# Three-bank score tiles and values in four column groups, in a two-layer transformer on one Trainium2 core

## The chip, the cores and the metric

The kernel runs on one core of a Trainium2 chip. Its engines work from queues of their own: TensorE (PE) multiplies matrices into PSUM, ScalarE (ACT) computes activations, VectorE (DVE) does elementwise work, GpSimd (POOL) copies and clears, SyncE (SP) starts DMAs. The metric is the device time of one execution in microseconds, lower is better. "Start to start" below is the distance of two neighbouring instructions of one engine.

## The reference

All inputs are bfloat16. `x` is 2048 x 512; attention has 32 heads of 16; the feed-forward width is 1792. The same weights are used in both layers.

```python
def A(x, wqkv, wo):                 # B=1, S=2048, D=512, H=32, Dh=16
    q, k, v = split(x @ wqkv)       # (H, S, Dh) each
    p = softmax(q @ k.T * Dh ** -0.5)
    return concat_heads(p @ v) @ wo

def B(x, w1, w2):
    return silu(x @ w1) @ w2

for layer in range(2):
    x = x + A(layernorm(x), wqkv, wo)
    x = x + B(layernorm(x), w1, w2)
return x
```

## The kernel before

Everything lies in SBUF. The 2048 queries are worked in four chunks of 512 (`c`), heads in eight blocks of four (`hb`), keys in 16 tiles of 128 (`kt`). A unit is one `(c, hb, kt)`: 512 in a layer.

For a unit, `emit_s` issues four score matmuls (L520). The four heads of a block lie at partitions 32j to 32j+16 of `KT` and `QT`, 17 rows each, the 17th holding a bound that keeps the exponent small; so the four use four row groups of the array. They write two PSUM tiles of two banks (`wide`, three such tiles in turn). ACT takes each tile with one exponential of 128 x 1024 into `p_sb` (L585). `emit_pv` then issues four value matmuls (L532), one for each head, all adding into one bank `o_ps`: the stationary operand is 128 columns wide and zero but for the head's 17 (16 of V and a column of ones that sums the exponentials). These padded operands, `vd`, are filled by POOL copies (L141), four for every four key tiles. After 16 key tiles DVE copies `o_ps` to `oT` (L573), and a step transposes it back and divides by the sums (`heads_piece`, L336 to L343).

All else in attention is a side step: K and Q of the next head block (`k_piece` L225, `q_piece` L298 to L327), the output projection of the last chunk (`epilogue_pieces` L362, L371), its feed-forward (`ffn_pieces`: L392, tanh L429, gate L430, L399) and the next layer's normalising and V (`next_pieces`, L269). A step has at most two matmuls of 512 columns or four transposes; they share one PSUM bank (`narrow`). A list `Pump` holds the steps, and after each unit some are issued, as many as it takes to be done by the end of the chunk. PE, ACT and DVE run in the order in which the program is written (`manual_schedule`).

The order in a unit is: exponentials of this unit, scores of the next, values of the last half and this first half, side steps. ACT and PE wait for each other through the score tiles.

Ahead of layer 0 stand the normalising, K of block 0, its maximum and Q, and all of V, one after another. Behind each layer's attention the last chunk's projection and feed-forward (`ffn_last`) run by themselves, and behind layer 0 the last chunk's normalising and V, and K of block 0 for all of layer 1.

Of the kernel before, what the change touches and what calls it, by code (L numbers as in the profile page):

```python
# [18 lines left out]
def kernel(  # L19
# [10 lines left out]
    nc = tc.nc  # L30
# [11 lines left out]
    NQC = S // 512  # L42
# [5 lines left out]
    NG = 4  # L48
    NR = 2
# [4 lines left out]
    xnpool = ctx.enter_context(tc.tile_pool(name="xnpool", bufs=2))  # L54
    xtpool = ctx.enter_context(tc.tile_pool(name="xtpool", bufs=4))
    vpool = ctx.enter_context(tc.tile_pool(name="vpool", bufs=2))
    qpool = ctx.enter_context(tc.tile_pool(name="qpool", bufs=3))
    qwork = ctx.enter_context(tc.tile_pool(name="qwork", bufs=1))
    ppool = ctx.enter_context(tc.tile_pool(name="ppool", bufs=5))
# [5 lines left out]
    spool = ctx.enter_context(tc.tile_pool(name="spool", bufs=3, space=bass.MemoryType.PSUM))  # L65
# [3 lines left out]
    def wide(name):  # L69
        return spool.tile([P, 2, 512], FP32, name=name, tag="s")  # L70
# [27 lines left out]

    x_sb = xpool.tile([P, TT, D], BF16, name="x_sb")
    for c in range(NQC):  # L100
        nc.sync.dma_start(
            x_sb[:, 4 * c : 4 * c + 4, :],
            xf[512 * c : 512 * (c + 1), :].rearrange("(tt p) d -> p tt d", p=P),
        )
# [22 lines left out]
    amax = xpool.tile([P, HB], FP32, name="amax")  # L127
    vs = [vpool.tile([P, TT, D], BF16, name=f"v{i}", tag="v") for i in range(2)]
    vdq = []
    for i in range(NR):  # L130
        vd = xpool.tile([P, NG, 4, P], BF16, name=f"vd{i}")
        nc.gpsimd.memset(vd[:], 0.0)
        for j in range(4):
            nc.gpsimd.memset(vd[:, :, j, 32 * j + DH : 32 * j + DH + 1], 1.0)
        vdq.append(vd)


    def vd_fill(va, hb, g, slot):
        for j in range(4):
            h = 4 * hb + j  # L140
            nc.gpsimd.tensor_copy(  # L141
                out=vdq[slot][:, :, j, 32 * j : 32 * j + DH],
                in_=va[:, NG * g : NG * (g + 1), DH * h : DH * (h + 1)],
            )
# [7 lines left out]
    def ln_rstd_act(mvb, rstd, n):  # L152
        std = small.tile([P, n, 1], FP32, name="std", tag="std")
        nc.scalar.activation(std[:], mvb[:, :, 1:2], ACT.Sqrt, bias=eps_t[:], scale=1.0)
        nc.vector.reciprocal(rstd[:], std[:])

    def ln_rstd(mvb, rstd, n):
        va = small.tile([P, n, 1], FP32, name="va", tag="va")
        nc.vector.tensor_scalar_add(out=va[:], in0=mvb[:, :, 1:2], scalar1=float(EPS))
# [6 lines left out]
            out=rstd[:].bitcast(I32), in0=sh[:], scalar1=-1.0, scalar2=float(0x5F3759DF),  # L166
# [4 lines left out]
        for _ in range(3):  # L171
            nc.vector.scalar_tensor_tensor(
                out=t1[:], in0=rstd[:], scalar=-0.5, in1=rstd[:], op0=ALU.mult, op1=ALU.mult
            )
            nc.vector.tensor_tensor(out=t2[:], in0=t1[:], in1=va[:], op=ALU.mult)
            nc.vector.scalar_tensor_tensor(
                out=rstd[:], in0=t2[:], scalar=1.5, in1=rstd[:], op0=ALU.add, op1=ALU.mult
            )
# [9 lines left out]
    def transpose_tile(xn, xnT, tq, wide_ps=False):  # L188
        if wide_ps:
            t_ps = spool.tile([P, CT, P], BF16, name="t4_ps", tag="s")  # L190
        else:
            t_ps = gpool.tile([P, CT, P], BF16, name="t_ps", tag="g")
        for ct in range(CT):
            nc.tensor.transpose(t_ps[:, ct, :], xn[:, ct * P : (ct + 1) * P], ident[:, :])  # L194
        nc.vector.tensor_copy(out=xnT[:, :, tq * P : (tq + 1) * P], in_=t_ps[:, :, :])


    def ln_steps(c, cell, act_sqrt=False, wide_ps=False):
        def stats(pair):
            if pair == 0:  # L200
                cell["mvb"] = small.tile([P, 4, 2], FP32, name="mvb", tag="mvb")
                cell["rstd"] = small.tile([P, 4, 1], FP32, name="rstd", tag="rstd")
            for i in (2 * pair, 2 * pair + 1):
                ln_stats(cell["mvb"], i, 4 * c + i)

        def rs():
            if act_sqrt:
                ln_rstd_act(cell["mvb"], cell["rstd"], 4)
            else:
                ln_rstd(cell["mvb"], cell["rstd"], 4)  # L210
            cell["xn0"] = ln_apply(cell["mvb"], cell["rstd"], 0, 4 * c)

        def tr(tq):
            if tq == 0:
                cell["xnT"] = xtpool.tile([P, CT, 512], BF16, name="xnT", tag="xt")
            if tq < 3:
                cell[f"xn{tq + 1}"] = ln_apply(cell["mvb"], cell["rstd"], tq + 1, 4 * c + tq + 1)
            transpose_tile(cell[f"xn{tq}"], cell["xnT"], tq, wide_ps)

        return [[lambda: stats(0), lambda: stats(1), rs]] + [[lambda tq=tq: tr(tq)] for tq in range(4)]  # L220


    def k_mm(xnT, hb, ps, cts):
        for ct in cts:
# [3 lines left out]
                rhs=xnT[:, ct, :],  # L228
# [4 lines left out]
    def k_piece(xnTs, c, hb):  # L233
        cell = {}

        def a():
            cell["ps"] = narrow("k_ps")
            k_mm(xnTs[c], hb, cell["ps"][:, :], (0, 1))

        def b():  # L240
            k_mm(xnTs[c], hb, cell["ps"][:, :], (2, 3))
            nc.vector.tensor_scalar(  # L242
                out=KT[:, hb, c * 512 : (c + 1) * 512], in0=cell["ps"][:, :],
                scalar1=onescol[:, 0:1], scalar2=None, op0=ALU.add,
            )
# [3 lines left out]
    def k_two(xnTs, c, hb):  # L249
        k_ps = wide("k2_ps")  # L250
        for i in range(2):
            k_mm(xnTs[c + i], hb, k_ps[:, i, :], range(CT))
        nc.vector.tensor_scalar(
            out=KT[:, hb, c * 512 : (c + 2) * 512],
            in0=k_ps[:].rearrange("p a b -> p (a b)"),
            scalar1=onescol[:, 0:1], scalar2=None, op0=ALU.add,
        )

    def amax_bm(hb):
        nc.vector.tensor_reduce(  # L260
            out=amax[:, hb : hb + 1], in_=KT[:, hb, :], axis=AX.X, op=ALU.max,
            apply_absolute_value=True,
        )
        nc.vector.tensor_scalar_mul(out=Bm[:, hb, :], in0=E[:, :], scalar1=amax[:, hb : hb + 1])

    def v_mm(xnT, tt, ps, cts):
        tq = tt % 4
        for ct in cts:
            nc.tensor.matmul(  # L269
                ps, lhsT=xnT[:, ct, tq * P : (tq + 1) * P], rhs=wv_sb[:, ct, :],  # L270
                start=(ct == 0), stop=(ct == CT - 1),
            )

    def v_piece(cellx, tt, va):
        cell = {}

        def a():
            cell["ps"] = narrow("v_ps")
            v_mm(cellx["xnT"], tt, cell["ps"][:, :], (0, 1))

        def b():
            v_mm(cellx["xnT"], tt, cell["ps"][:, :], (2, 3))
            nc.vector.tensor_copy(out=va[:, tt, :], in_=cell["ps"][:, :])

        return [a, b]

    def v_two(xnT, tt, va):
        ps = wide("v2_ps")
        for i in range(2):
            v_mm(xnT, tt + i, ps[:, i, :], range(CT))  # L290
        nc.vector.tensor_copy(out=va[:, tt : tt + 2, :], in_=ps[:, :, :])

    def q_piece(xnTs, c, hb, QTs):
        cell = {}

        def mm(cts):
            for ct in cts:
                nc.tensor.matmul(  # L298
                    cell["ps"][:, :],
                    lhsT=wq_pad[:, ct, 4 * hb : 4 * hb + 4, :].rearrange("p h s -> p (h s)"),  # L300
                    rhs=xnTs[c][:, ct, :],
# [8 lines left out]
        def b():  # L310
            mm((2, 3))
            qc = qwork.tile([P, 512], BF16, name="qc", tag="qc")
            nc.vector.tensor_copy(out=qc[:], in_=cell["ps"][:, :])  # L313
            qu = qwork.tile([P, 512], BF16, name="qu", tag="qu")
            nc.vector.tensor_scalar(
                out=qu[:].bitcast(I16), in0=qc[:].bitcast(I16), scalar1=0x7FFF, scalar2=None,
                op0=ALU.bitwise_and,
            )
            cell["qu"] = qu

        def d():
            nc.tensor.matmul(  # L322
                cell["ps"][:, :], lhsT=Bm[:, hb, :], rhs=cell["qu"][:], start=False, stop=True,
                skip_group_check=True,
            )
            QTs[c][hb] = qpool.tile([P, 512], BF16, name="QT", tag="qt")
            nc.vector.tensor_copy(out=QTs[c][hb][:], in_=cell["ps"][:, :])  # L327

        return [a, b, d]


    def heads_piece(oT, hb, attn):
        def a():
            at_ps = gpool.tile([P, 4, 4, 32], BF16, name="at_ps", tag="g")
            for tq in range(4):
# [6 lines left out]
            nc.vector.reciprocal(rec[:], at_ps[:, :, :, DH : DH + 1])  # L342
            nc.vector.tensor_tensor(  # L343
                out=attn[:, :, 64 * hb : 64 * hb + 64].rearrange("p t (j d) -> p t j d", j=4),
                in0=at_ps[:, :, :, 0:DH],
                in1=rec[:].to_broadcast([P, 4, 4, DH]),
# [5 lines left out]


    def epilogue_pieces(c, attn):
        pieces = []
        for tq in range(4):
# [23 lines left out]
            def pc(tq=tq, cell=cell, mm=mm):  # L380
                mm((2, 3))
                tt = 4 * c + tq
# [7 lines left out]
    def h_mm(xfT, ft, ps, cts):  # L390
        for ct in cts:
            nc.tensor.matmul(  # L392
                ps, lhsT=w1_sb[:, ct, ft * P : (ft + 1) * P], rhs=xfT[:, ct, :],
# [290 lines left out]
```

## Time and profile before

| | us |
|---|---|
| timed runs | 2185.21, 2188.16 (median), 2188.69 |
| span of the profiled execution | 2190.4 |
| to the first exponential | 65.2 |
| attention of layer 0 | 1006.1 |
| last exponential of layer 0 to first of layer 1 | 89.9 |
| attention of layer 1 | 968.3 |
| last exponential to the end | 60.8 |

The profiled execution is listed by its span, from its first instruction to its last; no other time of it is given. It lies 2.2 us above the median of the timed runs. In the page a line of a group gives the engine, the operation, the tiles, shapes and count, then the busy time, the mean duration of one in ns, and the engine's idle time ahead of it with what ended it. A duration counts from issue, so neighbouring ACT or PE instructions overlap in it: 2048 exponentials of 1237 ns are 1920 us busy. `PEclk` is the clock that TensorE was granted, in tenths of full speed for 40 slices of the span. A timeline line has the start, the time to the last end, engine, line and operation, and a count where several were merged. A stretch line has its two ends, its length, the time PE was busy with the count of matmuls, the granted clock, and the DMA share and rate.

### The profile page before, as it was taken

The numbers are of one execution on the slowest core, as the hardware profiler recorded it, in microseconds if no ns is written. First come the engines' busy times: TensorE is split into PE (matmuls) and PEld (weight loads), VectorE is DVE, ScalarE is ACT, GpSimd is POOL, SyncE is SP. The second block draws the span as 40 slices with busy tenths as digits, with TensorE's granted clock in tenths as the row PEclk, the third lists the DMA queues.
The fourth block names the chain that finished last, engine by engine and source line by source line (L and its number), as shares of the span: only waits on it lengthen the run. The fifth ranks groups of instructions, "written<-read, shape, count | busy, mean of one in ns | idle before, by whom it ended". The sixth has DMA issues, their size and how long they took to land.

```text
span 2190.4 us, 28490 instructions
## 1 busy us (share of the span) xinstructions
PE 1952.9 (89%) x10355; PEld 717.0 (33%) x10561; DVE 558.6 (26%) x1106; ACT 1943.4 (89%) x2152; POOL 248.2 (11%) x1055
## 2 busy tenths in 40 slices
PE   3999988999889998899778999998999989998996
PEld 1333323333333333333222333333333333333332
DVE  6323212112311133112343323131113111131114
ACT  0899989999799997999517999999999999999981
POOL 3111101111011110111000111111111111111100
PEclk9999999999899998999878999999999999999997
DMA  4000000000000000000000000000000000000000
GB/s 144 1 1 1 1 1 1 1 1 1 1 1 1 1 1 1 1 1 1 1 0 1 1 1 1 1 1 1 3 8 1 1 1 8 4 1 1 6 5 10
DMA packets 8477, 11.79 MB, mean 5 GB/s; under 512 B 400, under 2 KB 7312, under 8 KB 8336
## 3 DMA queue, kind: packets, MB, share of 16 engines
q1 hardware_dynamic: 7280, 8.39, 1.1%
q8 instruction: 82, 1.34, 0.3%
q10 hardware_dynamic: 1056, 1.57, 0.2%
q14 instruction: 59, 0.48, 0.1%
HBM read 7.86 MB, written 2.10 MB: 5 GB/s over the span
## 4 chain that ended last, share of the span: by engine, by line
PE 64%; ACT 21%; issue 8%; DVE 6%; DMA 0%; ACTq 0%; DVEq 0%
PE o_ps L532 30%; ACT p_sb L585 19%; PE s_ps L520 17%; PE y_ps L399 3%; PE k_ps L225 3%; PE q_ps L298 3%; PE h_ps L392 2%; PE y_ps L371 2%; PE v_ps L269 2%; ACT t_sb L429 1%; DVE st L149 1%; PE t_ps L194 1%; DVE oT L573 1%; PE at_ps L336 1%; DVE hT L477 1%
## 5 line engine op out<-in xcount | busy, mean ns | idle before, releaser
L585 ACT ACTIVATE p_sb<-s_ps 128x1024 bf16<-128x1024 f32 x2048 | 1920.4, 1237 | 123.3 <-PE s_ps L520 123.3
L532 PE MATMUL o_ps<-p_sb,vd 128*128 128x512 bf16 x3909 | 1045.1, 386 | 19.7 <-issue 15.5
L520 PE MATMUL s_ps<-QT,KT 17*128 17x512 bf16 x4096 | 575.3, 385 | 89.6 <-ACT p_sb L585 85.3
L532 PEld LDWEIGHTS <-vd 128*128 128x128 bf16 x4096 | 318.8, 98 | 484.8 <-issue 246.8
L141 POOL COPY vd<-v 128x64 bf16<-128x64 bf16 x1024 | 231.5, 239 | 1868.1 <-PE o_ps L532 1723.6
L520 PEld LDWEIGHTS <-KT 17*128 17x128 bf16 x4096 | 175.1, 91 | 591.1 <-issue 571.2
L573 DVE CAST oT<-o_ps 128x512 bf16<-128x512 f32 x64 | 44.3, 692 | 380.3 <-PE o_ps L532 380.3
L430 DVE SCALAR_TENSOR_TENSOR hT<-t_sb,h_ps 128x512 bf16<-128x512 f32 x84 | 57.5, 684 | 301.5 <-ACT t_sb L429 301.5
L399 PE MATMUL y_ps<-w_sb,hT 128*128 128x512 bf16 x445 | 128.0, 388 | 5.4 <-DVE hT L477 4.5
L392 PE MATMUL h_ps<-xnT,w_sb 128*128 128x512 bf16 x438 | 126.6, 387 | 3.2 <-DVE hT L477 1.4
L313 DVE CAST qc<-q_ps 128x512 bf16<-128x512 f32 x64 | 44.2, 691 | 173.0 <-PE q_ps L298 173.0
L242 DVE TENSOR_SCALAR KT<-k_ps,onescol 128x512 bf16<-128x512 f32 x56 | 42.0, 750 | 172.1 <-PE k_ps L225 172.1
L194 PE MATMUL t_ps<-ident,xn 128*128 128x128 bf16 x256 | 32.2, 271 | 57.1 <-DVE xn L182 55.4
L405 DVE SCALAR_TENSOR_TENSOR x_sb<-y_ps,x_sb 128x512 bf16<-128x512 f32 x32 | 22.1, 690 | 232.7 <-PE y_ps L399 232.7
L476 ACT ACTIVATE t_sb<-h_ps 128x1024 f32<-128x1024 f32 x14 | 14.3, 1024 | 75.1 <-PE h_ps L392 59.0
L298 PE MATMUL q_ps<-xnT,wq_pad 128*128 128x512 bf16 x255 | 77.0, 385 | 2.5 <-DVE attn L343 2.4
L225 PE MATMUL k_ps<-xnT,wk_pad 128*128 128x512 bf16 x254 | 78.7, 402 | 0.3 <-issue 0.2
L429 ACT ACTIVATE t_sb<-h_ps 128x512 f32<-128x512 f32 x84 | 76.9, 916 | 0.0
L399 PEld LDWEIGHTS <-hT 128*128 128x128 bf16 x448 | 44.3, 100 | 61.4 <-issue 6.1
L392 PEld LDWEIGHTS <-w_sb 128*128 128x128 bf16 x448 | 44.7, 100 | 58.4 <-issue 8.3
L327 DVE CAST QT<-q_ps 128x512 bf16<-128x512 f32 x64 | 44.2, 691 | 37.0 <-PE q_ps L322 37.0
L371 PE MATMUL y_ps<-wo_sb,aT 128*128 128x512 bf16 x126 | 40.8, 425 | 7.5 <-DVE aT L366 7.3
(58 smaller groups left out, 572.8 us busy)
## 6 DMA issues: line engine op xcount, KB each, us to landing
w_sb<-in_B_w_dram SPq DMA_DIRECT2D x2, 1792.0 KB, 15.0
x_sb<-in_A_x_dram SPq DMA_DIRECT2D x4, 512.0 KB, 9.8
out_dram<-x_sb SPq DMA_DIRECT2D x16, 128.0 KB, 1.7
wraw<-in_A_wqkv_dram ACTq DMA_DIRECT2D x1, 1024.0 KB, 7.6
wv_sb<-in_A_wqkv_dram ACTq DMA_DIRECT2D x1, 512.0 KB, 10.0
wo_sb<-in_A_wo_dram SPq DMA_DIRECT2D x1, 512.0 KB, 12.3
```

The lines of the kernel that those rows point to most:

```text
L141: nc.gpsimd.tensor_copy(out=vdq[slot][:, :, j, 32 * j : 32 * j + DH], in_=va[:, NG * g : NG * (g + 1), DH * h : DH * (h + 1)],)
L225: nc.tensor.matmul(ps, lhsT=wk_pad[:, ct, 4 * hb : 4 * hb + 4, :].rearrange("p h s -> p (h s)"), rhs=xnT[:, ct, :], start=(ct == 0), stop= ...
L298: nc.tensor.matmul(cell["ps"][:, :], lhsT=wq_pad[:, ct, 4 * hb : 4 * hb + 4, :].rearrange("p h s -> p (h s)"), rhs=xnTs[c][:, ct, :], star ...
L371: nc.tensor.matmul(cell["ps"][:, :], lhsT=cell["aT"][:, ct, :], rhs=wo_sb[:, ct, :], start=(ct == 0), stop=(ct == CT - 1),)
L392: nc.tensor.matmul(ps, lhsT=w1_sb[:, ct, ft * P : (ft + 1) * P], rhs=xfT[:, ct, :], start=(ct == 0), stop=(ct == CT - 1),)
L399: nc.tensor.matmul(ps, lhsT=hT[:, ft, tq * P : (tq + 1) * P], rhs=w2_sb[:, ft, :], start=(ft == 0), stop=(ft == FT - 1),)
L429: nc.scalar.activation(t_sb[:, 0, :], hc["ps"][:, :], ACT.Tanh, scale=0.5)
L430: nc.vector.scalar_tensor_tensor(out=cell["hT"][:, ft, :], in0=t_sb[:, 0, :], scalar=1.0, in1=hc["ps"][:, :], op0=ALU.add, op1=ALU.mult,)
L520: nc.tensor.matmul(tiles[j // 2][:, j % 2, :], lhsT=KT[32 * j : 32 * j + VS, hb, kt * P : (kt + 1) * P], rhs=QT[32 * j : 32 * j + VS, :], ...
L532: nc.tensor.matmul(o_ps[:, :], lhsT=vdq[kt // NG % NR][:, kt % NG, j, :], rhs=p_sb[:, jj, :], start=(kt == 0 and j == 0), stop=(kt == TT - ...
L573: nc.vector.tensor_copy(out=oT[:], in_=o_ps[:])
L585: nc.scalar.activation(p_sb[:].rearrange("p a b -> p (a b)"), s_now[pr][:].rearrange("p a b -> p (a b)"), ACT.Exp, scale=float(SCALE),)
```

## The change

- A score tile has three banks (`NB = 3`), and there are two tiles. The banks of all units stand in one row, and a run is three of them, so units and runs don't line up: 1366 runs in all. ACT takes 128 x 1536 at a time.
- V is kept in 17-column blocks with the ones already in place (`va`), and a head's 32 columns of it are the stationary operand; each of the four heads writes its own 32 partitions of `o_ps`. `vd` and its POOL copies are gone; instead POOL sets both `va` to ones at the start.
- A unit's four value matmuls are issued together, a run behind its last exponential.
- The opening works chunk by chunk: ACT normalises (Identity with scale and bias), K of block 0 and V of that chunk follow, and ACT copies V out of PSUM. V of the last four key tiles is left to side steps.
- In layer 0's last chunk, K of block 0 for the first three chunks of layer 1, part of its maximum and layer 1's first Q become side steps; only the last chunk's K stays behind the layer. V of the last chunk is a side step of layer 1.
- Q's bias gets a PSUM tile of its own and is added on DVE.
- `ffn_last` takes tanh and gate by 512 in place of 1024, and its output in the narrow bank in place of one of three.
- One side step is issued after a run in place of one or two after a unit, counted by the runs left in the chunk.

Chunks stay at 512 queries (`CH`). The core of the diff:

```diff
-    NG = 4
-    NR = 2
+    NB = 3
+    RUN = 1
+    CH = [4, 4, 4, 4]
...
-    spool = ctx.enter_context(tc.tile_pool(name="spool", bufs=3, space=bass.MemoryType.PSUM))
+    spool = ctx.enter_context(tc.tile_pool(name="spool", bufs=6 // NB, space=bass.MemoryType.PSUM))
...
-    for i in range(NR):
-        vd = xpool.tile([P, NG, 4, P], BF16, name=f"vd{i}")
-        nc.gpsimd.memset(vd[:], 0.0)
...
+    VW = VS * H + 32 - VS
+    vs = []
+    for i in range(2):
+        va = xpool.tile([P, TT, VW], BF16, name=f"va{i}")
+        nc.gpsimd.memset(va[:], 1.0)
+        vs.append(va)
...
+    def q_bias(c, hb, cell, QTs):
+        n = CH[c] * P
+        qc = cell["qc"]
+        qu = qwork.tile([P, 512], BF16, name="qu", tag="qu")
+        nc.vector.tensor_scalar(
+            out=qu[:, 0:n].bitcast(I16), in0=qc[:, 0:n].bitcast(I16), scalar1=0x7FFF,
+            scalar2=None, op0=ALU.bitwise_and,
+        )
+        ps = narrow("qb_ps")
+        nc.tensor.matmul(
+            ps[:, 0:n], lhsT=Bm[:, hb, :], rhs=qu[:, 0:n], start=True, stop=True
+        )
+        QTs[c][hb] = qpool.tile([P, 512], BF16, name="QT", tag="qt")
+        nc.vector.tensor_tensor(
+            out=QTs[c][hb][:, 0:n], in0=ps[:, 0:n], in1=qc[:, 0:n], op=ALU.add
+        )
...
+    def emit_s(tiles_, banks, QTs):
+        for kk in range(max(nk(b[0]) for b in banks)):
+            for i, (c, hb, g, j) in enumerate(banks):
...
+                nc.tensor.matmul(
+                    tiles_[i // NB][:, i % NB, kk * n : (kk + 1) * n],
+                    lhsT=KT[32 * j : 32 * j + VS, hb, kt * P : (kt + 1) * P],
+                    rhs=QTs[c][hb][32 * j : 32 * j + VS, 0:n],
+                    start=True,
+                    stop=True,
+                )
+
+    def emit_pv(o_ps, unit, ps, va):
...
+            for j in range(4):
+                h = 4 * hb + j
+                nc.tensor.matmul(
+                    o_ps[32 * j : 32 * j + 32, 0:n],
+                    lhsT=va[:, kt, VS * h : VS * h + 32],
+                    rhs=ps[j][:, kk * n : (kk + 1) * n],
+                    start=(kt == 0),
+                    stop=(kt == TT - 1),
+                )
...
+    for c in range(G4):
+        for i in range(4):
+            xn = xnpool.tile([P, D], BF16, name="xn", tag="xn")
+            nc.scalar.activation(
+                xn[:], x_sb[:, 4 * c + i, :], ACT.Identity,
+                bias=cells[c]["nmr"][:, i, :], scale=cells[c]["rstd"][:, i, :],
+            )
+            cells[c][i] = xn
+        if c + 1 < G4:
+            p_stats(c + 1)
+        for i in range(4):
+            transpose_tile(cells[c][i], xT, 4 * c + i, wide_ps=True)
+        if c + 1 < G4:
+            p_rstd(c + 1)
+        k_ps = narrow("k0_ps")
+        k_mm(0, 512 * c, 512, k_ps[:, :], range(CT))
+        k_out(0, 512 * c, 512, k_ps[:, :])
+        if c + 1 < G4:
+            for tt in range(4 * c, 4 * c + 4):
+                v_ps = wide("v2_ps")
+                v_mm(tt, v_ps[:, 0, :], range(CT))
+                nc.scalar.copy(v_dst(vs[0], tt), v_ps[:, 0, :].rearrange("p (h d) -> p h d", d=DH))
...
+        banks = [u + (j,) for u in units for j in range(4)]
+        per = NB * RUN
+        runs = [banks[i : i + per] for i in range(0, len(banks), per)]
...
+            if not last and c == NCH - 1 and hb == 2:
+                t_end = T0[c] * P
+                for t in range(0, t_end, 512):
+                    pump.add([k_piece(0, t, min(512, t_end - t))])
+                pump.add([[lambda: amax_part(0, 0, 0, t_end)]])
+                pump.add([q_pre(0, 0, q0, "q0")])
...
+        for r, bk in enumerate(runs):
...
+                nc.scalar.activation(
+                    p_sb[:, 0:w, :].rearrange("p a b -> p (a b)"),
+                    s_ps[:, 0:w, :].rearrange("p a b -> p (a b)"),
+                    ACT.Exp,
+                    scale=float(SCALE),
+                )
...
+                s_now = alloc_s(r + 1)
+            values(ready)
+            ready |= set(done_now)
...
+            later = sum(4 for _ in range(hb + 1, HB))
+            total = pump.steps()
+            todo = -(-(total + later) // left_of[r]) if total else 0
+            pump.some(todo)
...
+        if not last:
+            c = NCH - 1
+            run(ln_steps(c, lambda: xT_view(c), wide_ps=True))
+            n = CH[c] * P
+            k_ps = wide("kl_ps")
+            k_mm(0, T0[c] * P, n, k_ps[:, 0, 0:n], range(CT))
+            k_out(0, T0[c] * P, n, k_ps[:, 0, 0:n])
+            amax_part(0, 1, T0[c] * P, S)
+            bm_make(0, two=True)
```

## The prediction

> **What bounds the kernel now.** I read the page first, then the timeline of ScalarE, then TensorE's, then the table by stretches of time. The page:
>
> ```profile
> span 2190.4 us, 28490 instructions
> ...
> PE 1952.9 (89%) x10355; PEld 717.0 (33%) x10561; DVE 558.6 (26%) x1106; ACT 1943.4 (89%) x2152; POOL 248.2 (11%) x1055
> ...
> PEclk9999999999899998999878999999999999999997
> ...
> L585 ACT ACTIVATE p_sb<-s_ps 128x1024 bf16<-128x1024 f32 x2048 | 1920.4, 1237 | 123.3 <-PE s_ps L520 123.3
> L532 PE MATMUL o_ps<-p_sb,vd 128*128 128x512 bf16 x3909 | 1045.1, 386 | 19.7 <-issue 15.5
> ```
>
> PE and ACT are both 89% busy, so neither share decides. By the timeline ACT runs exponentials from 65.2 to 1071.4 and from 1161.3 to 2129.6: attention is 1974.4 us, the rest 216.0 (opening 65.2, middle 89.9, tail 60.8). ACT's own price, in its timeline:
>
> ```profile
> 1476.74 5.88 ACT L585 ACTIVATE p_sb<-s_ps 128x1024 bf16<-128x1024 f32 x6
> 1482.17 0.95 ACT L429 ACTIVATE t_sb<-h_ps 128x512 f32<-128x512 f32 x1
> 1482.65 5.97 ACT L585 ACTIVATE p_sb<-s_ps 128x1024 bf16<-128x1024 f32 x6
> ```
>
> Six exponentials take 5.43 us from start to start, 0.905 each; the 512-wide tanh takes 0.48. So 2048 x 0.905 + 84 x 0.48 = 1894 of the 1974 is ACT work and 80 is waiting for scores. Why it waits is on TensorE, at full and at half clock:
>
> ```profile
> 709.29 0.50 PE L520 MATMUL s_ps<-QT,KT 17*128 17x512 bf16 x4
> 709.73 1.04 PE L532 MATMUL o_ps<-p_sb,vd 128*128 128x512 bf16 x4
> 710.60 0.59 PE L392 MATMUL h_ps<-xnT,w_sb 128*128 128x512 bf16 x2
> 711.13 0.50 PE L520 MATMUL s_ps<-QT,KT 17*128 17x512 bf16 x4
> ```
> ```profile
> 569.07 0.61 PE L520 MATMUL s_ps<-QT,KT 17*128 17x512 bf16 x4
> 569.62 1.89 PE L532 MATMUL o_ps<-p_sb,vd 128*128 128x512 bf16 x4
> ```
>
> Start to start at full clock: scores 0.44 (0.32 where both halves were ready), four value matmuls 0.87 (0.217 each), a two-matmul side step 0.53; together 1.84 against two exponentials' 1.81. At half clock the scores take 0.55, a value matmul 0.42, and a side step 0.98 (from 1162.90 to the scores at 1163.87). The table of stretches, cut where the granted clock changes, which is always a multiple of 3.413 us:
>
> ```profile
> 561.42:564.83 3.41, 1.65 (x13) 1.00 0.03 5
> 564.83:568.25 3.42, 2.61 (x7) 0.50 0.00 0
> 568.25:571.66 3.41, 3.11 (x13) 0.50 0.00 0
> 571.66:575.07 3.41, 2.54 (x15) 1.00 0.00 0
> ...
> 588.73:592.14 3.41, 1.54 (x8) 1.00 0.00 0
> 592.14:595.55 3.41, 3.00 (x15) 0.50 0.02 5
> ```
>
> After a thinly filled stretch the clock is halved for the next, and it comes back after a dense one. I put a number on it from the starts in the trace: a 512-column matmul streams 0.213 us at full clock, twice that at half; a group of scores counts 0.3, transposes 1.1; the filled share is multiplied by the clock. In 628 of the 629 stretches after 45 us the next one has full clock exactly if this **filling** is 0.38 or more (the nearest drop came after 0.378, the nearest return after 0.380). Value matmuls are what keeps the present kernel above: without side steps it fills about 0.5 (0.87 + 0.3 x 0.21 of 1.83 us).
>
> **The change part by part.** *Three-bank tiles.* 4096 banks go in 1366 exponentials of 1536. The slope between 512 and 1024 is 0.427 per 512, so one takes 0.905 + 0.427 = 1.33: 1820 in place of 1853, -34. Bounds: 1.5 x 0.905 = 1.36 (no gain), and by the slope less a tenth 1.29 (-90); I take the slope. With the tanhs attention is 1860 at least.
>
> *Values in four column groups.* A unit's four matmuls write 32 partitions each. No such matmul is in the trace. The nearest row is the scores, four row groups that start 3 ns apart: 0.32 to 0.44 a group at full clock, 0.55 at half; the other bound is today's one behind another, 0.87 and 1.7. I take the scores' price, since nothing but the direction of the split differs. POOL's 1024 copies (231 us) go; nothing on the path waited for them, 0.
>
> *Per exponential* TensorE then has three scores, 0.75 of a values group and at most one side step. Full clock: 0.44 + 0.33 + 0.53 = 1.30, just under 1.33. Half clock: 0.55 + 0.41 + 0.98 = 1.94. Two tiles in place of three leave some 0.8 us (one exponential less the scores' 0.5) to absorb a burst.
>
> *What is late next: the clock.* At the exponentials' pace a run of 1.33 us is filled by 0.16 (values) + 0.06 (scores), a share of 0.17, without a side step, and to 0.50 with one of two matmuls (0.43 more). In the feed-forward's first half (steps of two, two and no matmuls, with a tanh, 4.47 us) it is (0.86 + 3 x 0.22) / 4.47 = 0.34. So the clock is halved wherever the queue is empty, and in that half. At half clock a run with a side step lasts 1.94 and fills 0.65 / 1.94 = 0.34: still under 0.38, so it does not come back by itself; the best-placed stretch (two values groups, two side steps, one scores group in 3.41 us) reaches 0.386, so now and then it does.
>
> Price of half clock throughout: two-matmul side steps number 350 in layer 0 and 318 in layer 1 (K 56, Q 64 and 62, V 32 and 8, output projection 24, FFN 84 + 84, next K 6), 668. In the 84 FFN triples TensorE needs 2 x 1.94 + 0.96 = 4.84 against 4.47: 84 x 0.37 = 31. The other 500 lose 0.61 each, 305. Another 186 steps (heads, Q's bias, transposes), which wait for DVE's 0.69 copy or its kind, lose about 0.4: 74. Slack of 0.78 at each of 64 head blocks: -50. Sum 360. Some stretches regain the clock; I give the two-matmul steps 30% of their loss back, -92: **+268** (bounds: 170 if half of it all is regained, 400 if DVE's copies hold TensorE for another 40).
>
> [...]
>
> [...]
>
> *Opening.* Normalising moves to ACT, V's evacuation to ACT, its last four tiles into the queue. POOL clears two value arrays of 8944 columns, 8.2 us each by the 1.87 of a 2048 one: the first, from about 13.6, ends near 21.8, and ACT's V copies, with the next chunk's normalising behind them, wait for it. First chunk to about 25, two more at 9 (ACT 4 x 0.6, transposes and copy 1, K 1, V 3.5, copy 0.6), the last 5, then max, Q and scores 5.5: 54, -11. Between -16 and +2; I take -10.
>
> *Moved steps.* Layer 1's K and Q for the first head block, and V's last four tiles, join a queue that has some 145 steps at most for a chunk's 171 runs; they issue no DMA, and SP's and POOL's queues keep their order. They cost nothing at full clock, and are counted above at half. The values of tiles 12 to 15 force V's last steps at run 16 at the latest; 12 steps are done by run 12, so no wait.
>
> *Middle.* Now: V 1140.0 to 1149.6 (9.6), K to the last copy 6.1, max and scale 2.5, Q's copy 0.7. After: no V, K of one chunk 2.7, max of 512 about 1.0, no Q copy; wide transposes 1.2 shorter: -17. The last FFN pays: 14 tanh and gate pairs in turn through one tile, 1.42 each (tanh 0.6, gate 0.69, two hand-overs) for 7 x 2.37, +3.3, less 1 for an earlier start, and one bank for the output, 3 x 0.95. +5 here and +5 in the tail. So the rest is 216 - 10 - 12 + 5 = 199.
>
> Sum: 1860 + 268 + 10 (starts of blocks) + 199 = 2337 on the 2190.4 of the profiled execution, which is 2.2 above the median of the timed runs; rounded, **2340**.
>
> **The rivals.** *The clock stays up* (faster). It decides if a values group counts more than about 1.2 full matmuls on the average of a chunk: at the exponentials' pace a chunk takes 170.7 x 1.33 + 14 x 0.48 = 234 us and needs 0.38 x 234 = 89 of filling and has 44 from side steps (88 x 0.43, transposes and Q's bias 6), 11 from scores and 128 x 0.216 = 28 from values. For it: no row shows what a column group counts, and four streams enter at once. Against it: four row groups count only 0.3. Then ACT bounds: 1860 + 199 + 30 to 60 of waits = 2090 to 2120; 2100.
>
> *The column groups run one behind another.* Clock full; a run with a side step takes 0.44 + 0.65 + 0.53 = 1.62: 500 x 0.29 + 186 x 0.25 - 50 = 141, and 20 of stalls: 2220 (2150 to 2290). For it: the values' matmuls share all 128 rows, and scores, which overlap, do not. Against it: they write different partitions and hold different columns. It is the case in which the change doesn't do what it says.
>
> **How the numbers follow.** Half clock in most of attention 0.55 (2240 to 2470), clock up 0.33 (2070 to 2130), one behind another 0.12. The likeliest gives 2340. About 0.2% can be told from no change. Faster: 0.32 + 0.02; the same 0.03, where terms cancel; slower 0.63. The range leaves out the lower third of the clock-up case and the end of permanent half clock: 2085 to 2440; it has a gap between 2130 and 2150.
>
> **What would show it.** Right: granted clock 5 to 7 in the slices of attention where it is 9 now; exponentials x1366 at 1.33 spacing only where the queue is empty, 1.9 beside K and the output half of the FFN; idle of ACT before `p_sb` put down to PE's scores, several hundred us. Values groups of four starting within some 0.1 us show that the split works; 0.2 apart is the second rival. Wrong: clock 9 in attention and ACT idle below 80 us, which would mean that a column group counts for more than it fills; or an exponential of 1536 far from 1.33. The first exponential should start at 50 to 60, the layers' gap should be 70 to 85.

## The result, and the profile after

The changed kernel takes 2392.2 us (median of four runs, 2383.6 to 2411.7) against 2186.7 (2184.6 to 2188.7): 1.095 times the time before, 95% interval 1.090 to 1.100. The forecast was 2340, in a range of 2085 to 2440, with 0.63 on slower. The profiled execution lasted 2395.5. By the starts and ends of the exponentials:

| us | before | after | forecast |
|---|---|---|---|
| to the first exponential | 65.2 | 58.5 | 55 |
| attention, both layers | 1974.4 | 2160.0 | 2138 |
| last exponential of layer 0 to first of layer 1 | 89.9 | 94.8 | 78 |
| last exponential to the end | 60.8 | 82.2 | 66 |
| granted clock in attention, layer 0, layer 1 | 0.98, 0.99 | 0.59, 0.56 | "5 to 7" |

The page of the changed kernel:

```profile
span 2395.5 us, 25305 instructions
...
PE 2052.9 (86%) x10561; PEld 483.8 (20%) x10561; DVE 550.0 (23%) x1110; ACT 1972.7 (82%) x1512; POOL 27.6 (1%) x23
...
PEclk8555655675557755585565665555555575557657
...
L700 ACT ACTIVATE p_sb<-s_ps 128x1536 bf16<-128x1536 f32 (+1 forms) x1366 | 1896.2, 1504 | 264.7 <-PE s_ps L535 259.4
...
L550 PE MATMUL o_ps<-p_sb,va 128*32 128x512 bf16 x4096 | 595.8, 571 | 1.0 <-ACT p_sb L700 1.0
```

The value matmuls' busy time fell from 1045 to 596 us, and TensorE as a whole is busier than before: 2053 against 1953. `PEclk` points to why: the digits of attention are 5 to 7, once 8, where they were mostly 9. ACT now idles 265 us ahead of its exponentials (259 of it put down to the scores), 123 before.

TensorE's timeline, first at full and then at half clock (start, time to the last end, operation, count):

```profile
502.57 0.39 PE L535 MATMUL s_ps<-QT,KT 17*128 17x512 bf16 x3
502.90 0.40 PE L550 MATMUL o_ps<-p_sb,va 128*32 128x512 bf16 x4
503.23 0.60 PE L403 MATMUL y_ps<-w_sb,hT 128*128 128x512 bf16 x2
503.92 0.39 PE L535 MATMUL s_ps<-QT,KT 17*128 17x512 bf16 x3
```
```profile
527.97 0.61 PE L535 MATMUL s_ps<-QT,KT 17*128 17x512 bf16 x3
528.50 0.62 PE L550 MATMUL o_ps<-p_sb,va 128*32 128x512 bf16 x4
529.05 1.03 PE L253 MATMUL v_ps<-wv_sb,xT 128*128 128x512 bf16 x2
530.02 0.61 PE L535 MATMUL s_ps<-QT,KT 17*128 17x512 bf16 x3
```

Four column groups cost 0.33 at full clock and 0.55 at half: they overlap. A run with four values and a step takes 1.35 at full clock, the exponential's own pace; at half it takes 2.05. ACT's timeline where the queue of steps is empty, with the clock halved too:

```profile
846.43 24.31 ACT L700 ACTIVATE p_sb<-s_ps 128x1536 bf16<-128x1536 f32 x18 [0.25 <-PE s_ps L535]
```

The granted clock in the same stretch (0.50):

```profile
846.40:871.00 24.60, 19.35 (x117) 0.50 0.00 1
```

Eighteen in (24.31 - 1.45) / 17 = 1.345 from start to start, where 1.330 is the least: here the halved clock by itself costs ACT next to nothing. The stretches around the drop at 511.28 (ends, length, PE busy and count, granted clock):

```profile
504.45:507.86 3.41, 2.97 (x20) 1.00 0.00 0
507.86:511.28 3.42, 2.54 (x23) 1.00 0.00 0
511.28:514.69 3.41, 2.34 (x17) 0.50 0.00 0
518.10:521.52 3.42, 3.42 (x25) 0.50 0.02 5
```

The prediction's filling is nearly 0.5 in the first (the clock stays) and some 0.3 in the second: one Q's bias, the transposes of a head block, two groups of values and three of scores. From 511.3 the clock is halved for 160 us on end, though TensorE never rests for more than 2.2. In the last line it is busy without a gap by the profile's records, and the clock does not come back: the busy time is scores, values and transposes, and fills some 0.3.

TensorE's timeline in the last feed-forward shows what the forecast of the tail missed:

```profile
2340.50 1.87 PE L384 MATMUL h_ps<-fx,w_sb 128*128 128x512 bf16 x4 [0.52 <-DVE fx L184]
2343.78 1.86 PE L384 MATMUL h_ps<-fx,w_sb 128*128 128x512 bf16 x4 [1.41 <-DVE hT L394]
2347.05 3.57 PE L384 MATMUL h_ps<-fx,w_sb 128*128 128x512 bf16 x8 [1.41 <-DVE hT L394]
```

The matmuls of a tile's second and third bank wait for the gate (DVE, `hT`) of the bank before. Before the change, 39 of these matmuls stood in one piece:

```profile
2155.51 10.43 PE L392 MATMUL h_ps<-xnT,w_sb 128*128 128x512 bf16 x39 [0.52 <-DVE xnT L195]
```

### The profile page after: what moved, and what is told of

The parts are those of the page before. It is cut to its first block, busy times and chain, and to the rows that moved or that the text cites. A ratio compares the mean times of both kernels' runs of the same rounds, so it can differ in the third digit from the quotient of the medians.

```text
span 2395.5 us, 25305 instructions
## 1 busy us (share of the span) xinstructions
PE 2052.9 (86%) x10561; PEld 483.8 (20%) x10561; DVE 550.0 (23%) x1110; ACT 1972.7 (82%) x1512; POOL 27.6 (1%) x23
## 4 chain that ended last, share of the span: by engine, by line
PE 57%; ACT 23%; issue 11%; DVE 8%; POOL 0%; DMA 0%; ACTq 0%; POOLq 0%; DVEq 0%
ACT p_sb L700 22%; PE s_ps L535 16%; PE o_ps L550 13%; PE h_ps L384 8%; PE k_ps L211 4%; PE y_ps L403 4%; PE q_ps L281 4%; PE y_ps L362 3%; PE v_ps L253 2%; PE qb_ps L310 1%; DVE st L143 1%; PE at_ps L329 1%; PE t_ps L183 1%; DVE oT L661 1%; ACT t_sb L393 1%
## 5 line engine op out<-in xcount | busy, mean ns | idle before, releaser
L700 ACT ACTIVATE p_sb<-s_ps 128x1536 bf16<-128x1536 f32 (+1 forms) x1366 | 1896.2, 1504 | 264.7 <-PE s_ps L535 259.4
L535 PE MATMUL s_ps<-QT,KT 17*128 17x512 bf16 x4096 | 774.7, 560 | 160.9 <-ACT p_sb L700 150.9
L550 PE MATMUL o_ps<-p_sb,va 128*32 128x512 bf16 x4096 | 595.8, 571 | 1.0 <-ACT p_sb L700 1.0
L384 PE MATMUL h_ps<-fx,w_sb 128*128 128x512 bf16 x448 | 213.6, 594 | 31.8 <-DVE hT L394 30.2
L550 PEld LDWEIGHTS <-va 128*32 128x32 bf16 x4096 | 113.6, 100 | 418.5 <-issue 418.5
L211 PE MATMUL k_ps<-xT,wk_pad 128*128 128x512 bf16 x252 | 118.7, 574 | 8.9 <-DVE KT L220 4.0
L281 PE MATMUL q_ps<-xT,wq_pad 128*128 128x512 bf16 x256 | 117.7, 564 | 6.8 <-DVE attn L336 3.7
L329 PE MATMUL at_ps<-ident,oT 128*128 128x128 bf16 x256 | 35.4, 286 | 26.2 <-DVE oT L661 21.6
L253 PE MATMUL v_ps<-wv_sb,xT 128*128 128x512 bf16 x128 | 53.4, 542 | 2.0 <-ACT va L606 1.0
L314 DVE TENSOR_TENSOR QT<-qb_ps,qc 128x512 bf16<-128x512 f32 x64 | 44.3, 692 | 40.3 <-PE qb_ps L310 40.3
L310 PE MATMUL qb_ps<-qu,Bm 128*128 128x512 bf16 x64 | 34.5, 539 | 21.2 <-DVE qu L305 20.3
```

Source lines behind the costliest of these rows:

```text
L211: nc.tensor.matmul(ps, lhsT=wk_pad[:, ct, 4 * hb : 4 * hb + 4, :].rearrange("p h s -> p (h s)"), rhs=xT[:, ct, t0 : t0 + n], start=(ct == ...
L253: nc.tensor.matmul(ps, lhsT=xT[:, ct, tt * P : (tt + 1) * P], rhs=wv_sb[:, ct, :], start=(ct == 0), stop=(ct == CT - 1),)
L281: nc.tensor.matmul(cell["ps"][:, 0:n], lhsT=wq_pad[:, ct, 4 * hb : 4 * hb + 4, :].rearrange("p h s -> p (h s)"), rhs=xT[:, ct, T0[c] * P : ...
L384: nc.tensor.matmul(ps[:, i * n : (i + 1) * n], lhsT=w1_sb[:, ct, ft * P : (ft + 1) * P], rhs=xfT[:, ct, 0:n], start=(ct == 0), stop=(ct == ...
L535: nc.tensor.matmul(tiles_[i // NB][:, i % NB, kk * n : (kk + 1) * n], lhsT=KT[32 * j : 32 * j + VS, hb, kt * P : (kt + 1) * P], rhs=QTs[c] ...
L550: nc.tensor.matmul(o_ps[32 * j : 32 * j + 32, 0:n], lhsT=va[:, kt, VS * h : VS * h + 32], rhs=ps[j][:, kk * n : (kk + 1) * n], start=(kt = ...
```

## The experiments

Parts of each profiled run, in us, with the granted clock in the two layers' attention:

| kernel | attention | outside | clock | median | ratio to before, 95% |
|---|---|---|---|---|---|
| before | 1974 | 216 | 0.98, 0.99 | 2187 | |
| changed | 2160 | 236 | 0.59, 0.56 | 2392 | 1.090 to 1.100 |
| padded_three | 2065 | 228 | 0.97, 0.98 | 2295 | 1.048 to 1.052 |
| groups_unit_runs | 2052 | 220 | 0.65, 0.62 | 2269 | 1.034 to 1.040 |
| padded_unit_runs | 1989 | 216 | 0.98, 1.00 | 2206 | 1.006 to 1.011 |
| groups_fill_two | 2082 | 229 | 0.80, 0.89 | 2322 | 1.057 to 1.068 |
| last_ffn_reordered | 2152 | 206 | 0.59, 0.57 | 2365 | 1.079 to 1.082 |
| groups_unit_fill_three | 2003 | 200 | 0.95, 0.94 | 2206 | 1.006 to 1.010 |
| groups_fill_three | 1970 | 232 | 0.97, 0.98 | 2214 | 1.008 to 1.013 |
| groups_fill_narrow | 2122 | 235 | 0.80, 0.82 | 2385 | 1.087 to 1.103 |
| groups_fill_few_rows | 2367 | 237 | 0.59, 0.58 | 2607 | 1.188 to 1.198 |
| fill_three_mended | 1956 | 206 | 0.97, 0.97 | 2164 | 0.988 to 0.992 |
| fill_three_mended_wide | 1954 | 199 | 0.97, 0.97 | 2153 | 0.982 to 0.986 |

**Undoing the parts.** The first three undo the column groups, the three-bank tiles, and both.

padded_three:

```diff
-                    o_ps[32 * j : 32 * j + 32, 0:n],
-                    lhsT=va[:, kt, VS * h : VS * h + 32],
+                    o_ps[:, 0:n],
+                    lhsT=vdq[kt // NG % 2][:, kt % NG, j, :],
```

To make room for `vd`, V is stored 16 wide and there are two Q tiles in place of three.

> Three-bank score tiles as changed, values as before: 128 columns wide, zero but for 17, filled by POOL copies. Theory (the clock: a values group of four column groups fills TensorE as little as one matmul, so the filling falls under 0.38 and the clock is halved): four full matmuls a unit bring the clock back to 0.9 or more, at the price of 0.87 a unit in place of 0.33; a run with a side step takes 0.33 + 0.65 + 0.6 = 1.58 against 1.33, so some 2230 (2190 to 2290), under the changed kernel's 2392 although TensorE has more to do. Rival (the tiles: with two tiles of three banks ACT and PE wait for each other, whatever the clock): the added work comes on top, 2392 or more.

groups_unit_runs (and padded_unit_runs with both edits):

```diff
-    NB = 3
-    RUN = 1
+    NB = 2
+    RUN = 2
```

> Column groups as changed, but tiles of two banks, three of them, and runs of four banks (one unit), as before. Theory (the clock): filling stays under 0.38, granted clock below 0.75; TensorE at half clock needs 1024 x (0.55 + 0.55) + 668 x 0.98 + 186 x 0.6 = 1893 us of attention, as much as ACT's 1893, and the two don't overlap evenly: 2250 (2200 to 2330), slower than before. Rival (the tiles): the old tiles bring the old time back or better, 2190 or less.

> Both undone: two-bank tiles in runs of four banks, values 128 columns wide; what stays is the new opening, the next layer's K and Q as side steps, the last feed-forward by 512 and the spread of the steps. Both theories: attention as before, 1974 (1950 to 1990), clock 0.95 or more; the parts outside attention between before's 216 and the changed kernel's 235: 2190 (2165 to 2215).

The pages of padded_three and of groups_unit_runs:

```profile
PEclk8899999999999999998779999999999999999987
...
L724 ACT ACTIVATE p_sb<-s_ps 128x1536 bf16<-128x1536 f32 (+1 forms) x1366 | 1897.2, 1502 | 184.6 <-PE s_ps L551 178.1
L566 PE MATMUL o_ps<-p_sb,vd 128*128 128x512 bf16 x4096 | 1087.8, 389 | 1.4 <-ACT p_sb L724 0.4
```
```profile
PEclk8566656566566765587585665555675658555668
...
L550 PE MATMUL o_ps<-p_sb,va 128*32 128x512 bf16 x4096 | 566.1, 542 | 1.1 <-ACT p_sb L700 1.1
```

The groups alone pull the clock down, with either tile; taking them away brings it back. So the theory holds for the clock. In time the groups cost 97 us with three-bank tiles (2392 against 2295) and 63 with two-bank ones (2269 against 2206). The rival holds in part: the tiles cost 89 with padded values and 123 with groups. With padded values that is TensorE at full clock: the exponentials that started there were late by 213 us over 1.33 each (up to 40 of it tanhs), mostly beside a side step. A run with values and a step takes 1.72, not the 1.58 expected, which is why 2295 lies 5 over the range. Two-bank tiles with groups lose less than three-bank ones although their clock is low as well. That fits their third tile, but no run separates the number of tiles from their size. padded_unit_runs shows what the rest of the change is worth: 20 us lost, none of it outside attention on balance (a shorter opening and gap make up for the longer tail).

**Filling TensorE on purpose.** These four only add matmuls, of zeros into the bank of the values, so that the output stays:

```diff
+            load[0] = 0
             pump.some(todo)
+            if o_ps[0] is not None:
+                for _ in range(FILL - load[0]):
+                    nc.tensor.matmul(
+                        o_ps[0][:, :], lhsT=zero[:], rhs=w2_sb[:, 0, :],
+                        start=False, stop=False, skip_group_check=True,
+                    )
```

`load` counts the step's matmuls (a set of transposes as one). FILL is 2, and 3 in the second; in the third the added matmuls write `o_ps[0][0:32, :]` from `zero[:, 0:32]`, in the fourth they take `zero[0:32, :]` and `w2_sb[0:32, 0, :]`.

> The changed kernel, with matmuls added that change nothing: after a run whose side step has fewer than two matmuls, as many of 128 zero columns as are missing to two are added into the bank of the values. Theory (the clock): a run at full clock is then filled 0.22 + 0.43 in 1.33 us, 0.48, so the clock stays up where it is up (a run without a step takes 0.33 + 0.33 + 0.43 = 1.09, which still fits), but at half clock a run fills 0.65 / 1.81 = 0.36, so where it drops it comes back slowly; 2200 (2100 to 2330), faster than the changed kernel although work is added, granted clock over 0.7. Rival (the tiles, or too much work on TensorE): added work can't help; 2392 or more.

> The changed kernel with three-bank tiles, and matmuls of 128 zero columns up to three a run in place of two. Theory (the clock): a run at half clock now takes 0.55 + 0.41 + 1.28 + 0.1 = 2.34 and fills 0.86 / 2.34 = 0.37, at the gate, so the clock comes back sooner than with two, where 330 exponentials ran at half clock; but a run with a side step needs 0.33 + 0.25 + 0.6 + 0.22 = 1.40 at full clock against 1.33, some 900 x 0.07 = 63: 1857 + 63 + 60 + 228 = 2210 (2150 to 2300), clock 0.9. Rival (more work, no return of the clock): 2322 as with two, or more.

The pages with two and with three:

```profile
PEclk8899786877668786896777999679998799798887
...
L743 PE MATMUL o_ps<-w_sb,zero 128*128 128x512 bf16 x1204 | 431.4, 433 | 0.0
```
```profile
PEclk8899999999899999999679999999999999999987
...
L715 ACT ACTIVATE p_sb<-s_ps 128x1536 bf16<-128x1536 f32 (+1 forms) x1366 | 1876.6, 1544 | 112.4 <-PE s_ps L550 110.0
L743 PE MATMUL o_ps<-w_sb,zero 128*128 128x512 bf16 x2480 | 762.4, 387 | 0.0
...
L565 PE MATMUL o_ps<-p_sb,va 128*32 128x512 bf16 x4096 | 417.1, 397 | 0.0
```

2480 matmuls that compute nothing make the kernel 178 us faster. Of the 1366 exponentials 1125 start at half clock in the changed kernel, 336 with two added, 45 with three. As expected, two a run keep the clock but hardly bring it back (2322 is within the range, at its slow end: some 198 us are still lost at half clock); three do both. That the loss from 2392 to 2214 comes from the clock, and not from the tiles alone or from too much work on TensorE, is shown by these two.

> As the kernel with two added matmuls a run, but the added ones write 32 columns (one column group, 32 partitions) in place of 128. They take the same stream time. Theory A (what counts is the share of the array that is used, so one column group counts a quarter of a full matmul, four at once one): the filling of a run without a step is (0.22 + 2 x 0.053) / 1.33 = 0.25, under 0.38, clock about 0.6, and the added matmuls cost 0.85 a run at half clock: 2500 (2400 to 2620). Theory B (what counts is the time in which anything streams): as with full ones, clock 0.83 and 2322 (2280 to 2370).

> As the kernel with two added matmuls a run, but the added ones use 32 of the 128 rows (partitions of the operands) and all 128 columns. In the kernel that added matmuls of 32 columns and 128 rows the granted clock was 0.80 against 0.83 with full ones, so columns don't matter to the gate. Theory A (rows matter, which would be why four scores of 17 rows count only 0.3): the filling of a run without a step is (0.22 + 2 x 0.25 x 0.213) / 1.33 = 0.25, the clock stays near 0.6, and the added matmuls cost 0.85 a run at half clock: 2450 to 2620. Theory B (only the time in which something streams matters, and the scores' 0.3 has another reason): clock 0.8, 2320 to 2390.

```profile
PEclk8688967779979967775669997598976689785887
...
L743 PE MATMUL o_ps<-w_sb,zero 128*32 128x512 bf16 x1204 | 430.7, 432 | 0.0
```
```profile
PEclk8665556765558555575576555658555665565556
...
L743 PE MATMUL o_ps<-w_sb,zero 32*128 32x512 bf16 x1204 | 606.8, 591 | 0.0
```

Matmuls of 32 columns hold the clock (0.80) almost like full ones (0.83); of 32 rows they don't (0.595), and then their time is paid on top: 2607. With the weights of the prediction, and stretches sorted at 0.37, an added narrow matmul weighed as 1.0 accounts for 653 of 667 stretches, weighed as 0.3 for some 470. The one of 32 rows weighed as nothing to 0.3 accounts for some 710 to 720 of 739, as 1.0 for some 466.

The kernel with 32 rows is not as clean a test as its expectation takes it for. Its added matmuls use 32 of the 128 rows, and some start together with scores (both at 704.76 here):

```profile
704.76 0.60 PE L743 MATMUL o_ps<-w_sb,zero 32*128 32x512 bf16 x1
704.76 0.61 PE L550 MATMUL s_ps<-QT,KT 17*128 17x512 bf16 x2
705.16 0.63 PE L743 MATMUL o_ps<-w_sb,zero 32*128 32x512 bf16 x1
705.59 0.63 PE L550 MATMUL s_ps<-QT,KT 17*128 17x512 bf16 x1
```

606 of the 1204 start less than half a stream away from a score matmul; of the full and the narrow ones none does. So the matmuls of 32 rows don't all add streaming time. With those weighed as 0.3, the others weighed as 0.3 account for some 715 stretches, as 1.0 for some 690. So in these two kernels few rows count for little and few columns count nearly in full, but the first is shown less sharply than the second. It agrees with a values group of 128 rows counting 1. It fits the scores' 0.3 in direction only, since four groups of 17 rows at once use 68 of the 128 rows. The narrow kernel's 2385 is 15 above what theory B allowed (405 exponentials at half clock against 336); why it falls back a little more often was not settled.

**The wait in the last feed-forward.**

```diff
             for i, fts in enumerate(groups[g0 : g0 + NB]):
                 h_mm(fx, n, fts, h_ps[:, i, :], range(CT))
+            for i, fts in enumerate(groups[g0 : g0 + NB]):
                 h_act(hT, n, fts, h_ps[:, i, :])
```

> The changed kernel with one change of order in the last feed-forward of a layer: the matmuls of a tile's three banks are issued first, then the three tanhs and gates. In the changed kernel each bank's matmuls wait 1.41 us for the gate of the bank before it in the same tile, and the part from the first of these matmuls to the output's first took 35.8 us (1170.77 to 1206.52) against 15.4 before. Theory (the tail and the middle are long by this wait, not by the clock): 14 tanh and gate pairs at 1.42 are then the limit, some 22 us, so 13 less in each layer: tail 82 to 69, gap 95 to 82, 2366 (2355 to 2378). Rival (half clock alone makes them long): at half clock the matmuls take 14 x 1.71 = 24 and nothing overlaps better; 2385 or more.

The group in the page of this kernel, and then in that of groups_fill_three, where the order is the change's:

```profile
L384 PE MATMUL h_ps<-fx,w_sb 128*128 128x512 bf16 x448 | 196.7, 555 | 14.1 <-DVE hT L394 12.4
```
```profile
L397 PE MATMUL h_ps<-fx,w_sb 128*128 128x512 bf16 x448 | 146.1, 428 | 47.0 <-DVE hT L407 45.6
```

2365, as the theory had it: gap 81.8 (82 expected), tail 67.9 (69). Keeping the clock up in attention alone leaves the wait in place (46 us of idle time).

**Two-bank tiles with the clock kept.** `NB = 2`, `RUN = 2`, `FILL = 3` and the reordered feed-forward:

> Column groups, two-bank tiles in runs of four banks, the last feed-forward reordered as in the first kernel of this set, and matmuls of 128 zero columns up to three a run (side steps included). Theory (the clock, with filling 0.38 as the gate): at half clock a run of four banks and three full matmuls lasts 0.55 + 0.55 + 1.28 = 2.4 to 2.5 and fills (0.64 + 0.22 + 0.06) / 2.45 = 0.38, so the clock comes back, and at full clock it needs 0.33 + 0.33 + 0.75 = 1.4 of ACT's 1.81, so the matmuls cost nothing: attention 1893 + 40 to 80 of waits, the rest 220 - 20; 2150 (2110 to 2200), granted clock over 0.9, which is faster than both kernels. Rival (TensorE has no room for 2000 more matmuls): the time rises over the 2269 that the same tiles took without them.

The clock is at 0.93, the parts outside at 200 as expected, and the time fell by 63 from the 2269 without added matmuls. By the table 49 us of the fall are in attention; the other 20 lie outside it, where the feed-forward was reordered. But 2206 is 6 above the range: attention holds 152 us more than 2048 exponentials of 0.904 need. Tanhs are 40 of that, and exponentials that started at half clock or within a change of it are late by 70; why the clock still drops there was not followed.

**Mended.** From here on the kernels are meant to be fast. The new edits:

```diff
-        first = [[... for a in range(0, n, 2)] + [rs]]
+        first = [[... for a in range(0, n, 2)] + [rs] + [lambda: None] * (0 if wide_ps else 2)]
...
-        run(epilogue_pieces(NCH - 1, attns[NCH - 1]))
+        run(epilogue_pieces(NCH - 1, attns[NCH - 1], wide_ps=True))
```

> The kernel with matmuls added up to three a run (2213.7), with the two losses mended that its trace and the changed kernel's show: the last feed-forward issues the matmuls of a tile's banks before the tanhs and gates (27 less in the kernel where that was done alone), and two empty steps stand between a side step that starts the normalising's chain of small DVE operations and its first transposes, which waited about 1 us each for them in 29 runs. Theory (the clock was the loss, and these waits are the rest): 2214 - 27 - 20 = 2167 (2150 to 2185), faster than before by a little. Rival (the waits move on to the next step of the same chain, and the steps are late at the chunk's end): 2187, the same as before.

> As the other kernel of this set, and in the projection that runs by itself behind a layer the transposes get a PSUM tile of their own, so that they need not wait for DVE's addition to free the one bank (0.78 us a transpose group in the changed kernel, the next copy 0.42 behind it). Theory: 3 x 1.4 in each layer, 8 us less than the other kernel. Rival (DVE's copy and addition are the limit there): no difference over 2 us.

The page of the second:

```profile
span 2152.7 us, 29992 instructions
...
PEclk8799999999999999999779999999999999999998
...
L719 ACT ACTIVATE p_sb<-s_ps 128x1536 bf16<-128x1536 f32 (+1 forms) x1366 | 1878.1, 1539 | 95.0 <-PE s_ps L554 93.4
L747 PE MATMUL o_ps<-w_sb,zero 128*128 128x512 bf16 x2312 | 721.2, 387 | 19.3 <-issue 16.3
```

2164 and 2153: 1.0% and 1.6% faster than before; that is small, but both 95% intervals lie under 1. Attention fell by 14 us of the 20 expected for the empty steps, the parts outside by 27; the wide tile took another 11.5 in the medians (8 expected). All of the change stays in these kernels; 2312 matmuls of zeros keep the clock for it. No run puts the same mends on the old tiles and the padded values, so what groups and tiles are worth by themselves, once the clock is kept, stays open.

## Why the prediction was right

That the time lies within the range says little by itself: from 2085 to 2440 the range holds kernels that are faster and slower than before. What speaks for the prediction is that it named the mechanism, the halved clock, and priced it. The sum was 2337 for a profiled execution of 2395.5. Term by term:

- *The floor.* 1366 exponentials, 1.330 apart at the least, and 84 tanhs at 0.48 are 1857; the sum had 1860.
- *Column groups* overlap at the scores' price, as taken (0.33 and 0.55). The rival in which they run one behind another is out.
- *The clock term.* Attention is 303 us over the floor; the sum had 268 and 10 for starts of blocks. Divided over the exponentials by what TensorE did in each interval, tanhs taken out:

| interval | forecast | at half clock | at full clock |
|---|---|---|---|
| step of two matmuls, not FFN's first half | 500 x 0.61 = 305, less 92 | 344: 175 us, 0.51 each | 155: 0.6 us |
| FFN's first half | 31 | 180: 33 us | 18: 0 |
| heads, Q's bias, transposes | 74 | 142: 67 us | 26: 0.3 us |
| no step | 0 | 458: 1.4 us | 24: 0.1 us |
| steps of two kinds | not in the sum | 13: 20 us | 4: 5 us |
| slack at 64 head blocks | -50 | none seen | |

The mechanism and its parts were right: 155 of 499 two-matmul steps found the full clock, 31% where 30% was given. Two terms were mis-sized, and it is luck that they cancel in part. A two-matmul step lost 0.51, not 0.61. The slack of 50 is not there: it had been argued, not read from a row. (The lower bound of this term, half of the 360, is 180 and not 170.)

- *The filling rule.* With a values group as 1, scores 0.3, transposes 1.1, it tells 672 of 680 stretches (60 to 2380 us) with the limit at 0.37, and 665 at the 0.38 of the prediction. The 0.37 was chosen afterwards. The 0.213 us that 512 columns stream is half of the 0.426 from start to start at half clock; at full clock such matmuls start 0.216 apart.
- *The clock stays up* is out: the clock was halved in 84% of the stretches after 60 us, though the longest gap of TensorE in attention was 2.5 us. Before the change, too, half clock followed the stretch from 561.42, whose gaps are 0.8 us at most.
- *The last feed-forward* is the step of the sum that failed. The sum put +5 on each layer: 14 pairs of tanh and gate at 1.42 a pair, with the matmuls running ahead. They don't: in the diff, tanh and gate stand between the matmuls of one tile's banks, and each bank waits 1.41 us for the gate before it. The part from its first matmul to the output's first took 35.8 us against 15.4. So the tail is +21 and the gap +5 in place of -12; this is most of the 36 by which the parts outside (235.5 against 199) were too low (the reordered kernel wins back 27 of the gap and the tail). The wait could have been seen in the program beforehand, by asking of each tile who writes it next and what they wait for.
- *The opening* was 6.7 shorter, not 10. The `va` clearing took 7.5 us (8.2 estimated) and ACT's first copy came at 21.2 (21.8).

So floor -3, clock +25 and the parts outside +36 lead from 2337 to 2395.5.

## What to carry to other kernels

Before making TensorE's work cheaper, work out what keeps its clock: here work that was pure waste (zero columns) kept it at 0.97 and 0.98 in attention (padded_three), and without it, in the changed kernel, it was 0.59 and 0.56. The values' busy time fell by that from 1088 to 596 us, and TensorE's as a whole rose from 2003 to 2053. Where the traces show an engine at two clocks, price a saving on it twice, with all its other work at full and at half speed: a two-matmul step took 0.53 us and 0.98 before the change. Where ACT bounds and TensorE has room, as here, a few matmuls of zeros in runs that are thin can buy the clock back: 1125 exponentials started at half clock without them, 336 with two a run, 45 with three. And let no consumer stand between the writers of one tile's banks in program order, when the banks could have been filled first: here each bank waited 1.41 us, and the other order won 27.

## What the runs showed of the hardware

- In these runs the clock followed the rows in use far more than the columns: added matmuls of 32 columns held the clock at 0.80 (full ones 0.83), of 32 rows at 0.595. About half of the latter ran beside scores, so part of the difference can be streaming time that they did not add. Stationary operands of zeros hold the clock (0.97 and 0.98 in attention with three a run).
- Being busy is not enough: between 518.10 and 521.52 TensorE had no idle time in the profile's records, and the clock stayed halved.
- Column groups overlap: four matmuls of 32 columns, which start 3 ns apart, have their successor start after 0.33 us at full clock and 0.55 at half, where four padded ones took 0.87 at full.
